# Key and value rows in groups of nine tokens: 64-row matmul pairs for the kv sums of a linear attention with an MLP behind it

## The chip, the cores and the metric

The kernel runs on one core of one Trainium2 chip. The metric is the device time of the whole kernel in microseconds (us): the time before is 294.24 us, the median of three runs (293.79 to 294.32).

## The reference

All inputs and the output are float32. There are 8 batches, 8 heads, 576 tokens and a head width of 64; the MLP goes from 512 to 2048 and back to 512.

```python
B, H, S, D = q.shape                                  # 8, 8, 576, 64
theta = np.pi / 2.0 * np.arange(S) / S
phi(x) = concat([relu(x) * cos(theta), relu(x) * sin(theta)], axis=-1)   # 128 wide
kv  = einsum('bhsf,bhsd->bhfd', phi(k), v)
z   = sum(phi(k), axis=2)
num = einsum('bhsf,bhfd->bhsd', phi(q), kv)
den = einsum('bhsf,bhf->bhs', phi(q), z)[..., None] + 1e-06
x   = (num / den).transpose(0, 2, 1, 3).reshape(B * S, H * D)           # 4608 x 512
out = leaky_relu(x @ w_in, 0.01) @ w_out                                 # 4608 x 512
```

The kv sum runs over the tokens of one batch and head, in any order. It gives a 128 x 64 matrix; two columns of ones beside v (so 66 columns, `NE`) give z with it.

## The kernel before, in words

A batch has 576 = 512 + 64 tokens. The first 512 are the main part (`MAIN`): partition p holds the four tokens 4p to 4p+3 (`J = 4`), so that one load moves runs of 4 x 64 floats (1024 bytes). The last 64 are the tail: two heads lie on top of each other, one in partitions 0 to 63 and one in 64 to 127, and a tail is loaded in two halves, in runs of 256 bytes. So k and v of one batch take one main load (two halves for batches 0 and 1) and two tail loads each. The main loads go into the `stage` pool (seven buffers, shared with the loads of q and of the weights, which are cast to f16 from there), the tails of k and v into `kvtail` (four buffers). `kpm` and `kpt` (pool `kpp`, two buffers) hold phi(k) of main part and tail in f16; `vmain` and `vtail` hold v in f16, with the ones, in two copies that take turns.

phi is written half by half (`phi_half`): on VectorE (DVE, L226) one instruction does the max with 0 and the product with cos or sin, a column with one value for each partition; on ScalarE (ACT, L224) it is a Relu with a scale. `k_main` does one of the four tokens, cos and sin half, over all eight heads (512 elements in each partition) or four heads (256); `k_tail` does the tail. `v_main` and `v_tail` copy v to f16.

The kv sum has two forms. Batches 0 and 1 do it in halves of four heads (`kv_half`, `kv_mm`): for each pair of heads one matmul of the tail (128 rows, 132 columns, L264; the zeros of `vtail` keep the two heads apart) and eight of the main part (128 rows, 66 columns, L274). Batches 2 to 7 do it at once (`kv_all`): eight tail matmuls of 64 rows (L290), which take the upper and the lower partitions in turn and write to two PSUM banks, then 32 of 128 rows (L299). ACT copies the sum to `kv` (L306, L315). `num` multiplies phi(q) by it (L373, or in halves L409), DVE divides (`divide`: L384, L388, L389), and x is transposed to `xT`.

The MLP runs over groups of 512 tokens: eight groups are the main parts of the eight batches, the ninth holds the tails of q of all batches. `ffn1` (L452) makes a pair of 128-row blocks of the hidden layer with 8 matmuls of 512 columns into a PSUM buffer of `ps_h` (two buffers); ACT takes leaky relu of the pair into `g` (L460; pool of two buffers). `ffn2` (L475) multiplies by w_out; DVE or ACT copies the result to `osb`, and SyncE (SP) stores it.

The order is written out by hand; each engine works in the order of the code. From group 1's middle on, a list of units (ffn1 of the next group and ffn2 of this one in turn, at positions that count 16 to a group) is woven with steps at positions of their own (`at`, `weave`): a step is put out before the first unit whose position is not smaller. `kv_steps` puts the work on k and v and the kv sum there, `load_steps` the loads, `q_steps` phi of q with its transposes by DMA. All loads, stores and DMA transposes wait in SP's one queue, and each waits for the eighth DMA before it to land.

Of the kernel before, what the change touches and what calls it, by code (L numbers as in the profile page):

```python
# [14 lines left out]
J = 4  # L15


@with_exitstack
def kernel(
# [22 lines left out]
    assert TAIL == P // 2 and B * TAIL == MAIN  # L42
    NKC = DM // P
# [6 lines left out]
    def pool(name, bufs, space=None):  # L50
        kw = {"space": space} if space is not None else {}
        return ctx.enter_context(tc.tile_pool(name=name, bufs=bufs, **kw))
# [4 lines left out]
    kvtail = pool("kvtail", 4)  # L57
    qtail = pool("qtail", 2)
    kppool = pool("kpp", 2)
# [21 lines left out]
    def load_main(nm, src, b, parts=(0, 1)):  # L81

        if parts[0] == 0:
            st[nm, b] = stage.tile([P, H, J, D], dt.float32, name=f"{nm}st", tag="stage")
        lo, hi = 4 * parts[0], 4 * parts[-1] + 4
        nc.sync.dma_start(  # L86
            st[nm, b][:, lo:hi],
            src[b, lo:hi, 0:MAIN, :].rearrange("h (p j) d -> p h j d", j=J),
        )

    def load_kvtail(nm, src, b):

        t = kvtail.tile([P, H // 2, D], dt.float32, name=f"{nm}tl", tag="kvtail")
        v4 = src[b, :, MAIN:S, :].rearrange("(c o) p d -> o p c d", o=2)
        for o in range(2):
            nc.sync.dma_start(t[o * TAIL : (o + 1) * TAIL], v4[o])  # L96
        st[nm + "t", b] = t
# [9 lines left out]

    def load_k(b):
        load_main("k", k, b)
        load_kvtail("k", k, b)  # L110

    def load_v(b):
        load_main("v", v, b)
        load_kvtail("v", v, b)
# [31 lines left out]
    load_kvtail("k", k, 0)  # L146
    load_main("k", k, 0, (0,))
    load_kvtail("v", v, 0)
# [32 lines left out]
    pos = const.tile([P, J + 1], dt.float32, name="pos")  # L181
# [15 lines left out]
    cos_t = const.tile([P, J + 1], dt.float32, name="cos_t")  # L197
    sin_t = const.tile([P, J + 1], dt.float32, name="sin_t")
# [5 lines left out]
    ones = const.tile([P, H, J, 2], dt.float32, name="ones")  # L204
    nc.vector.memset(ones, 1.0)
    vmain, vtail = [], []
    for i in range(2):
        vm = const.tile([P, H, J, NE], dt.float16, name=f"vmain{i}")
        nc.vector.tensor_copy(vm[:, :, :, D:NE], ones)

        vt = const.tile([P, H // 2, 2, NE], dt.float16, name=f"vtail{i}")
        nc.gpsimd.memset(vt, 0.0)
        for o in range(2):
            sl = slice(o * TAIL, (o + 1) * TAIL)
            nc.vector.tensor_copy(vt[sl, :, o, D:NE], ones[sl, 0:4, 0, :])
        vmain.append(vm)
        vtail.append(vt)
# [18 lines left out]
    def kp_tiles(b):  # L236
        st["kpm", b] = kppool.tile([P, H, J, F], dt.float16, name="kpm")
        st["kpt", b] = kppool.tile([P, H // 2, F], dt.float16, name="kpt")

    def k_main(b, j, eng_c, eng_s, lo=0, hi=H):  # L240
        kpm, kst = st["kpm", b], st["k", b]
        for eng, t, f in ((eng_c, cos_t, 0), (eng_s, sin_t, D)):
            phi_half(
                eng, kpm[:, lo:hi, j, f : f + D], kst[:, lo:hi, j, :], t[:, j : j + 1]
            )

    def k_tail(b, eng_c, eng_s):
        kpt, kt, c = st["kpt", b], st["kt", b], J
        phi_half(eng_c, kpt[:, :, 0:D], kt, cos_t[:, c : c + 1])
        phi_half(eng_s, kpt[:, :, D:F], kt, sin_t[:, c : c + 1])  # L250

    def v_main(b, lo, hi, eng):
        copy(eng, vmain[b % 2][:, lo:hi, :, 0:D], st["v", b][:, lo:hi])

    def v_tail(b, eng):
        for o in range(2):
            sl = slice(o * TAIL, (o + 1) * TAIL)
            copy(eng, vtail[b % 2][sl, :, o, 0:D], st["vt", b][sl])

    def kv_mm(b, hg, ps):  # L260
        kpm, kpt = st["kpm", b], st["kpt", b]
        for cc in range(2):
            c = 2 * hg + cc
            nc.tensor.matmul(  # L264
                ps[:, 2 * cc * NE : 2 * (cc + 1) * NE],
                lhsT=kpt[:, c, :],
                rhs=vtail[b % 2][:, c].rearrange("p a e -> p (a e)"),
                start=True,
                stop=False,
            )  # L270
            for o in range(2):
                h = 2 * c + o
                for j in range(J):
                    nc.tensor.matmul(  # L274
                        ps[:, (2 * cc + o) * NE : (2 * cc + o + 1) * NE],
                        lhsT=kpm[:, h, j, :],
                        rhs=vmain[b % 2][:, h, j, :],
                        start=False,
                        stop=(o == 1 and j == J - 1),
                    )  # L280

    def kv_all(b):

        ps = psum("n", [P, 2, 512], dt.float32, "ps_kv")[:, :, 0 : 4 * NE]
        ps = ps.rearrange("p o (c e) -> p o c e", c=4)
        kpm, kpt = st["kpm", b], st["kpt", b]
        for c in range(H // 2):
            for o in range(2):
                sl = slice(o * TAIL, (o + 1) * TAIL)
                nc.tensor.matmul(  # L290
                    ps[:, o, c],
                    lhsT=kpt[sl, c, :],
                    rhs=vtail[b % 2][sl, c, o, :],
                    start=(c == 0),
                    stop=False,
                )
        for h in range(H):
            for j in range(J):
                nc.tensor.matmul(  # L299
                    ps[:, h % 2, h // 2],  # L300
                    lhsT=kpm[:, h, j, :],
                    rhs=vmain[b % 2][:, h, j, :],
                    start=False,
                    stop=(h >= H - 2 and j == J - 1),
                )
        nc.scalar.copy(kv[b].rearrange("p (c o) e -> p o c e", o=2), ps)  # L306

    def kv_half(b, hg, where, out=True):
        st["kvh", hg] = psum(where, [P, 4 * NE], dt.float32, "ps_kvh")
        kv_mm(b, hg, st["kvh", hg])  # L310
        if out:
            kv_half_out(b, hg)

    def kv_half_out(b, hg):
        nc.scalar.copy(  # L315
            kv[b][:, 4 * hg : 4 * hg + 4].rearrange("p h e -> p (h e)"), st["kvh", hg]
        )
# [213 lines left out]
    kp_tiles(0)  # L531
# [4 lines left out]
    k_tail(0, DVE, DVE)  # L536
    v_tail(0, POOL)
    k_main(0, 0, ACT, DVE, 0, 4)
    for j in range(1, J):
        k_main(0, j, DVE, DVE, 0, 4)  # L540
    v_main(0, 0, 2, DVE)
    v_main(0, 2, 4, ACT)
# [4 lines left out]
    kv_half(0, 0, "o")  # L547
    for j in range(J):
        k_main(0, j, ACT, DVE, 4, 8)
    num_half(0, 0, 0, "h")  # L550
    num_half(0, 1, 0, "n")
    v_main(0, 4, 6, ACT)
    v_main(0, 6, 8, POOL)
    idle(6)
    x_transpose_half(0, 0, 0)
    kv_half(0, 1, "o")
# [28 lines left out]
    load_kvtail("k", k, 1)  # L585
    load_kvtail("v", v, 1)
    load_main("k", k, 1, (0,))
    load_w2(3, 0, 2)
    load_main("v", v, 1, (0,))
    load_w2(3, 2, 4)  # L590
    load_main("k", k, 1, (1,))
    load_main("v", v, 1, (1,))
    load_main("q", q, 2)
    load_k(2)
    load_v(2)
# [18 lines left out]
    def at(pos, f, *args):  # L614
        steps.append((pos, lambda: f(*args)))
# [14 lines left out]
    kp_tiles(1)  # L630
    k_tail(1, DVE, DVE)
    v_tail(1, DVE)
    for j in range(J):
        k_main(1, j, DVE, DVE, 0, 4)
    cast_w2(3, DVE, 0, 2)
    v_main(1, 0, 2, DVE)
# [9 lines left out]
    v_main(1, 2, 4, ACT)  # L646
    kv_half(1, 0, "h")
    for j in range(J):
        k_main(1, j, ACT, DVE, 4, 8)
# [4 lines left out]
    v_main(1, 4, 6, POOL)  # L654
    v_main(1, 6, 8, ACT)
# [5 lines left out]
    kv_half(1, 1, "h")  # L661
# [41 lines left out]
    def kv_steps(b, start, step, mm, eng_v, n_act=0):  # L703
        at(start - 0.01, kp_tiles, b)
        at(start, k_tail, b, DVE, DVE)
        for i in range(J):
            at(start + (i + 1) * step, k_main, b, i, ACT if i < n_act else DVE, DVE)
        v0, dv = (start + 1.5 * step, 1) if b > 3 else (start + 3 * step, 0.1)
        at(v0, v_main, b, 0, 4, eng_v)
        at(v0 + dv, v_main, b, 4, 8, eng_v)  # L710
        at(v0 + 2 * dv, v_tail, b, eng_v)
        at(mm, kv_all, b)

    def load_steps(b, pk, pv, pq):
        at(pk, load_k, b)
        at(pv, load_v, b)
        at(pq, load_main, "q", q, b)
# [13 lines left out]
    kv_steps(2, 9.7, 0.5, 14, DVE, 2)  # L731
# [6 lines left out]
    kv_steps(3, 20, 0.7, 24, ACT)  # L738
# [3 lines left out]
    kv_steps(4, 28, 1.2, 34, ACT)  # L742
# [3 lines left out]
    for b in range(5, NG):  # L746
        base = 16 * (b - 2)
        if b < B:
            load_steps(b, base - 14.5, base - 13, base - 14.6)
            kv_steps(b, base - 8, 1.2, base - 2, ACT)  # L750
        else:
            for j in range(J):
                at(base - 11.5 + 2 * j, load_qtail, j)
        q_steps(b, base - 8, 2, 1)
        out_steps(b, base + 1, 2, 1.6)
# [32 lines left out]
```

## Time and profile before

| | |
|---|---|
| median of three runs | 294.24 us (293.79 to 294.32) |
| the profiled execution's own time | 293.82 us |
| its span in the profile | 292.0 us |
| TensorE (PE) matmuls | busy 286.4 us, 98%, 1958 instructions |
| VectorE (DVE) | busy 128.7 us, 44%, 328 instructions |
| ScalarE (ACT) | busy 118.4 us, 41%, 148 instructions |
| GpSimd (POOL) | busy 12.7 us, 4%, 24 instructions |
| DMA | 87909 packets, 56.93 MB |

The profiled execution takes 1.8 us more than its span, for what lies ahead of and behind it. It is 0.42 us under the median of the runs. Matmul durations in the profile overlap (a matmul of 512 columns is 379 ns long, but the next one starts 216 ns later), so PE's pace is read from the starts. The granted clock is full in all forty slices.

### The profile page before, as it was taken

To read this page: it belongs to the slowest core of one execution; us is meant where nothing else is said; L and a number is where in the kernel's file an instruction comes from. 1 tells how busy PE (TensorE), PEld (TensorE's weight loads), DVE (VectorE), ACT (ScalarE), POOL (GpSimd) and SP (SyncE) were. 2 spreads that over 40 slices of the span, in tenths; PEclk is the share of its full clock that TensorE was granted. 3 is DMA by queue.
4 is the path that set the end of the run, shared out by engine and by line. 5 is a ranking of instruction groups with operands and counts; after the bars stand their busy time and mean duration, and the time that the engine had idled before them with its cause. 6 is when DMAs were issued, how large, how long until landed. Compare 5 with 4: busy or idle time off the path is not lost.

```text
span 292.0 us, 4774 instructions
## 1 busy us (share of the span) xinstructions
PE 286.4 (98%) x1958; PEld 152.7 (52%) x1958; DVE 128.7 (44%) x328; ACT 118.4 (41%) x148; POOL 12.7 (4%) x24
## 2 busy tenths in 40 slices
PE   8999999999999999999999999999999999999995
PEld 3585556555555555455545554555445444444444
DVE  6931687926835816823562356333323310000011
ACT  6865266753544632632263226322222222222200
POOL 2264000000000000000000000000000000000000
PEclk9999999999999999999999999999999999999999
DMA  7999999999999999789584989504691051011133
GB/s 233 348 386 407 325 364 335 315 204 324 212 241 318 229 291 298 166 162 338 164 182 84 296 233 199 91 37 110 160 199 38 36 108 38 36 54 54 39 71 73
DMA packets 87909, 56.93 MB, mean 195 GB/s; under 512 B 55888, under 2 KB 80720, under 8 KB 87504
## 3 DMA queue, kind: packets, MB, share of 16 engines
q1 hardware_dynamic: 87808, 56.57, 71.0%
q8 instruction: 15, 0.25, 0.4%
q10 hardware_dynamic: 80, 0.07, 0.1%
q14 instruction: 6, 0.05, 0.1%
HBM read 36.70 MB, written 9.44 MB: 158 GB/s over the span
## 4 chain that ended last, share of the span: by engine, by line
PE 94%; DMA 2%; SPq 1%; ACT 1%; DVE 1%; issue 0%
PE ps_h L452 43%; PE ps_o L475 41%; PE ps_num L373 3%; PE ps_kv L299 2%; DMA vst<-in_v_dram 2%; PE ps_l L504 1%; SPq L96 1%; PE ps_xth L425 1%; PE ps_qt L363 1%; PE ps_numh L409 1%; SPq L86 1%; PE ps_kv L290 0%; PE ps_idle L166 0%; PE ps_kvh L274 0%; ACT qpT L232 0%; PE ps_xt L438 0%
## 5 line engine op out<-in xcount | busy, mean ns | idle before, releaser
L452 PE MATMUL ps_h<-xT,w 128*128 128x512 f16 (+1 forms) x592 | 142.8, 373 | 0.1
L475 PE MATMUL ps_o<-w,g 128*128 128x512 f16 x560 | 139.5, 379 | 0.0
L460 ACT ACTIVATE g<-ps_h 128x1024 f16<-128x1024 f32 x72 | 73.2, 1023 | 128.8 <-PE ps_h L452 128.8
L452 PEld LDWEIGHTS <-w 128*128 128x128 f16 x592 | 64.4, 114 | 52.3 <-issue 0.2
L475 PEld LDWEIGHTS <-g 128*128 128x128 f16 x560 | 54.2, 98 | 61.4
L234 DVE COPY osb<-ps_o 128x512 f32<-128x512 f32 x31 | 21.4, 690 | 77.1 <-PE ps_o L475 75.3
L384 DVE TENSOR_SCALAR den<-ps_num 128x8 f32<-128x8 f32 x28 | 4.6, 165 | 54.9 <-PE ps_num L373 54.9
L389 DVE TENSOR_TENSOR xs<-ps_num,rden 128x512 f16<-128x512 f32 x28 | 19.4, 691 | 1.2 <-DVE rden L388 0.2
L226 DVE TENSOR_SCALAR kpm<-kst,sin_t 128x512 f16<-128x512 f32 (+1 forms) x40 | 16.6, 429 | 1.1 <-DMA kst<-in_k_dram 1.1
L226 DVE TENSOR_SCALAR qp<-qst,cos_t 128x512 f16<-128x512 f32 (+1 forms) x34 | 15.5, 456 | 2.8 <-DMA qst<-in_q_dram 2.8
L226 DVE TENSOR_SCALAR qp<-qst,sin_t 128x512 f16<-128x512 f32 (+1 forms) x34 | 15.5, 456 | 0.0
L373 PEld LDWEIGHTS <-qpT 128*128 128x128 f16 (+1 forms) x256 | 10.6, 101 | 7.3 <-issue 1.7
L232 ACT CAST vmain<-vst 128x1024 f16<-128x1024 f32 (+1 forms) x14 | 12.5, 920 | 2.4 <-DMA vst<-in_v_dram 2.3
L226 DVE TENSOR_SCALAR kpm<-kst,cos_t 128x512 f16<-128x512 f32 (+1 forms) x29 | 13.1, 453 | 0.3 <-DMA kst<-in_k_dram 0.3
L373 PE MATMUL ps_num<-kv,qpT 128*128 128x66 f16 (+1 forms) x256 | 11.8, 194 | 0.0
L166 PE MATMUL ps_idle<-blank 128*128 128x512 f16 x30 | 9.9, 478 | 1.2 <-DVE blank L161 1.2
L234 DVE CAST w<-w2st 128x1024 f16<-128x1024 f32 (+1 forms) x6 | 5.1, 868 | 11.8 <-DMA w2st<-in_moe_w_out_dram 11.8
L232 ACT COPY qpT<-ps_qt 128x1024 f16<-128x1024 f16 x7 | 7.0, 1012 | 5.7 <-PE ps_qt L363 5.7
L234 POOL CAST w<-w1st 128x1024 f16<-128x1024 f32 (+1 forms) x9 | 8.5, 945 | 3.6 <-DMA w1st<-in_moe_w_in_dram 3.6
L388 DVE RECIPROCAL rden<-den 128x8 f32<-128x8 f32 x36 | 7.3, 203 | 1.2
L299 PE MATMUL ps_kv<-vmain,kpm 128*128 128x66 f16 x192 | 7.1, 193 | 0.0
L299 PEld LDWEIGHTS <-kpm 128*128 128x128 f16 x192 | 6.4, 98 | 0.3
(62 smaller groups left out, 99.7 us busy)
## 6 DMA issues: line engine op xcount, KB each, us to landing
out_dram<-osb SPq DMA_DIRECT2D x32, 256.0 KB, 2.5
qst<-in_q_dram SPq DMA_DIRECT2D x7, 1024.0 KB, 6.8
kst<-in_k_dram SPq DMA_DIRECT2D x6, 1024.0 KB, 9.7
vst<-in_v_dram SPq DMA_DIRECT2D x6, 1024.0 KB, 9.4
w1st<-in_moe_w_in_dram SPq DMA_DIRECT2D x7, 512.0 KB, 10.4
w2st<-in_moe_w_out_dram SPq DMA_DIRECT2D x3, 1024.0 KB, 12.9
kst<-in_k_dram SPq DMA_DIRECT2D x4, 512.0 KB, 6.9
vst<-in_v_dram SPq DMA_DIRECT2D x4, 512.0 KB, 7.9
```

Of the source, the lines that this page charges most:

```text
L166: nc.tensor.matmul(ps, lhsT=blank[:, 0:P], rhs=blank)
L226: eng.tensor_scalar(out=o, in0=i, scalar1=0.0, scalar2=col, op0=ALU.max, op1=ALU.mult)
L232: nc.scalar.copy(o, i)
L234: eng.tensor_copy(o, i)
L299: nc.tensor.matmul(ps[:, h % 2, h // 2], lhsT=kpm[:, h, j, :], rhs=vmain[b % 2][:, h, j, :], start=False, stop=(h >= H - 2 and j == J - 1),)
L373: nc.tensor.matmul(ps[lo:hi, h // 4, (h % 4) * NE : (h % 4 + 1) * NE], lhsT=qpT[:, h, lo:hi], rhs=kv[b][:, h, :],)
L384: nc.vector.tensor_scalar_add(den.rearrange("p (a b) -> p a b", a=2), ps[:, :, D : 4 * NE : NE], 1e-6)
L388: nc.vector.reciprocal(rden, den)
L389: nc.vector.tensor_tensor(out=xs, in0=ps[:, :, 0 : 4 * NE].rearrange("p a (b e) -> p a b e", e=NE)[:, :, :, 0:D], in1=rden.rearrange("p (a ...
L452: nc.tensor.matmul(ps[:, m % 2, lo:hi], lhsT=w1[m // 4, c][0][:, w1[m // 4, c][1], m % 4 : 512 : 4], rhs=xT[:, lo // P : hi // P, c, :], s ...
L460: nc.scalar.activation(st["g", g][:, m - 1 : m + 1, :], ps, AF.Lrelu)
L475: nc.tensor.matmul(st["ps_o", g, tt], lhsT=st["g", g][:, m, tt * P : (tt + 1) * P], rhs=w2[:, m, :], start=(m == 0), stop=(m == NFT - 1),)
```

## The change

From batch 1 on, k and v have no main part and tail. 576 = 64 x 9, so partition p of 64 holds the nine tokens 9p to 9p+8 (`T = 9`), and the 128 partitions hold two heads on top of each other (`HP = 64`, `NC = 4` pairs of heads). One load moves runs of 9 x 64 floats (2304 bytes) for the whole batch; batch 1 has two halves of two pairs each. The tail loads of batches 1 to 7, their copies of v and their phi of k are gone.

phi of k is now done for each of nine tokens over four pairs (`k_token`: 256 elements), so 18 instructions for a batch in place of 8 of 512 and 2 of 256. Batch 1 does it another way: pair by pair, one DVE instruction for nine tokens (576 elements) with the table of cos or sin as a second tensor (`k_pair_half`), for pairs 0 and 1 and for the sin half of pairs 2 and 3; the cos half of pairs 2 and 3 goes token by token (128 elements), five on ACT and four on DVE. v is cast in two copies of 1152 elements a batch (four of 576 in batch 1) to `vm`, two copies that take turns.

`kv_sum` has for each pair of heads and each token two matmuls of 64 rows, upper and lower partitions, into two PSUM banks: 72 for a batch in place of 40 (batches 2 to 7) or 36 (batch 1, in two calls of 36 now).

`kpp` has one buffer in place of two, and the pool `kvtail` is gone: the tails of batch 0's k and v go through a buffer of `qtail`. Batch 0 keeps its form; its `kpm`, `kpt`, `vmain` and `vtail` lie in the first buffer of the pool of `g`, which group 1's hidden layer takes later. The stage buffers grow from 2048 to 2304 elements. Positions in `kv_steps` are set anew: nine steps of half the length in place of five.

```diff
+T = 9
-    kvtail = pool("kvtail", 4)
-    kppool = pool("kpp", 2)
+    kppool = pool("kpp", 1)
+    def load_kv(nm, src, b, parts=(0, 1)):
+        if parts[0] == 0:
+            st[nm, b] = stage.tile([P, NC, T, D], dt.float32, name=f"{nm}st", tag="stage")
+        sl = slice(2 * parts[0], 2 * parts[-1] + 2)
+        rows = src[b].rearrange("h s d -> (h s d)").rearrange("(c p x) -> p c x", c=NC, p=P)
+        nc.sync.dma_start(
+            st[nm, b][:, sl].rearrange("p c j d -> p c (j d)"), rows[:, sl]
+        )
...
+    scratch = gpool.tile([P, NFT, MAIN], dt.float16, name="g").rearrange("p m t -> p (m t)")
...
+    def k_token(b, j, eng, t, f, lo=0, hi=H // 2):
+        c = J + 1 + j
+        phi_half(
+            eng, st["kp", b][:, lo:hi, j, f : f + D], st["k", b][:, lo:hi, j, :],
+            t[:, c : c + 1],
+        )
...
+    def k_pair_half(b, c, t, f):
+        nc.vector.scalar_tensor_tensor(
+            out=st["kp", b][:, c, :, f : f + D],
+            in0=st["k", b][:, c],
+            scalar=0.0,
+            in1=t[:, J + 1 :][:, :, None].broadcast_to([P, T, D]),
+            op0=ALU.max,
+            op1=ALU.mult,
+        )
...
+    def kv_sum(b, lo, hi, where):
+        n = hi - lo
+        ps = psum(where, [P, 2, 512], dt.float32, "ps_kv")
+        for c in range(lo, hi):
+            for j in range(T):
+                for o in range(2):
+                    sl = slice(o * HP, (o + 1) * HP)
+                    nc.tensor.matmul(
+                        ps[:, o, (c - lo) * NE : (c - lo + 1) * NE],
+                        lhsT=st["kp", b][sl, c, j, :],
+                        rhs=vm[b % 2][sl, c, j, :],
+                        start=(j == 0),
+                        stop=(j == T - 1),
+                    )
...
-    load_kvtail("k", k, 1)
-    load_kvtail("v", v, 1)
-    load_main("k", k, 1, (0,))
+    load_kv("k", k, 1, (0,))
     load_w2(3, 0, 2)
-    load_main("v", v, 1, (0,))
+    load_kv("v", v, 1, (0,))
     load_w2(3, 2, 4)
...
-    v_main(1, 2, 4, ACT)
-    kv_half(1, 0, "h")
-    for j in range(J):
-        k_main(1, j, ACT, DVE, 4, 8)
+    v_pairs(1, 1, 2, ACT)
+    kv_sum(1, 0, 2, "h")
+    for c in range(2, 4):
+        k_pair_half(1, c, sin_t, D)
+    for j in range(T):
+        k_cos(1, j, ACT if j < 5 else DVE, 2, 4)
     ffn2_mm(0, 2, 12, 14)
...
     def kv_steps(b, start, step, mm, eng_v, n_act=0):
-        at(start - 0.01, kp_tiles, b)
-        at(start, k_tail, b, DVE, DVE)
-        for i in range(J):
-            at(start + (i + 1) * step, k_main, b, i, ACT if i < n_act else DVE, DVE)
-        v0, dv = (start + 1.5 * step, 1) if b > 3 else (start + 3 * step, 0.1)
-        at(v0, v_main, b, 0, 4, eng_v)
-        at(v0 + dv, v_main, b, 4, 8, eng_v)
-        at(v0 + 2 * dv, v_tail, b, eng_v)
-        at(mm, kv_all, b)
+        at(start - 0.01, kp_tile, b)
+        for j in range(T):
+            at(start + j * step, k_cos, b, j, ACT if j < n_act else DVE)
+            at(start + j * step, k_sin, b, j, DVE)
+        v0, dv = (start + 3 * step, 1) if b > 3 else (start + 6 * step, 0.1)
+        at(v0, v_pairs, b, 0, 2, eng_v)
+        at(v0 + dv, v_pairs, b, 2, 4, eng_v)
+        at(mm, kv_sum, b, 0, NC, "n")
...
-    kv_steps(2, 9.7, 0.5, 14, DVE, 2)
+    kv_steps(2, 9.7, 0.25, 14, DVE, 4)
```

## The prediction

> **What bounds the kernel now.** I read the page first (busy shares, granted clock), then the chain of waits, then the time line around one kv sum, and last the starts of single matmuls.
>
> ```profile
> PE 286.4 (98%) x1958; PEld 152.7 (52%) x1958; DVE 128.7 (44%) x328; ACT 118.4 (41%) x148; POOL 12.7 (4%) x24
> PEclk9999999999999999999999999999999999999999
> PE 94%; DMA 2%; SPq 1%; ACT 1%; DVE 1%; issue 0%
> L299 PE MATMUL ps_kv<-vmain,kpm 128*128 128x66 f16 x192 | 7.1, 193 | 0.0
> L299 PEld LDWEIGHTS <-kpm 128*128 128x128 f16 x192 | 6.4, 98 | 0.3
> ```
>
> PE is busy for 98% at full clock and makes up 94% of the chain. Busy alone would prove little, so I took the distance from each matmul's start to the next and subtracted what the same form takes when nothing interferes (216 ns for 512 columns, 56 for 128, about 32 for 66). Over the whole run 6.6 us are left over, of which 4.4 lie in the first 20 us (k, q and v of batch 0 landing), 0.53 between 40 and 50 us, 0.24 between 50 and 60, and 1.4 in all that follows. From 20 us to the end PE's stream is therefore nearly gapless, and the change costs what it adds to that stream, plus what it makes PE wait for. Faster loads can win only parts of those 0.8 us, since batch 0 is not touched.
>
> The time line of PE around the sum of batch 2, and the engines around it:
>
> ```profile
> 60.63 0.29 PE L290 MATMUL ps_kv<-vtail,kpt 64*128 64x66 f16 x8
> 60.85 1.19 PE L299 MATMUL ps_kv<-vmain,kpm 128*128 128x66 f16 x32
> 61.88 0.38 PE L452 MATMUL ps_h<-xT,w 128*128 128x512 f16 x1
> 54.69 1.94 ACT L460 ACTIVATE g<-ps_h 128x1024 f16<-128x1024 f32 x2
> 56.50 1.35 ACT L224 ACTIVATE kpm<-kst,cos_t 128x512 f16<-128x512 f32 x2
> 57.72 1.03 ACT L460 ACTIVATE g<-ps_h 128x1024 f16<-128x1024 f32 x1
> ```
>
> The first three lines show that the 64-row form is already there: eight tail matmuls in 0.22 us. The other three show ACT without a break from 54.69 to 58.75, which matters below.
>
> **The kv sums of batches 2 to 7, on the path.** Single starts of that sum, in ns after the regular place of the next matmul: 96 until the first tail matmul, then pairs of an upper and a lower one 3 or 4 ns apart, the pairs at 0, 38, 74 and 103; then 124 until the first 128-row matmul; then 31 distances between the 32, of which the first are 39, 35 and 33 and the long run is 32.2; 33 more to the next 512-column matmul. The two long distances, 96 and 124, are the change between 64 and 128 rows: about 90 ns more than a step each. All six sums agree within 5 ns, 1.35 us each.
>
> After it there are 36 pairs. The way in stays (96). The second change of form moves from between tail and main part to the end (124). Between lie 35 distances: the first three cost 103 as in the tails, the other 32 at 32.2 give 1030. The sum is 96 + 103 + 1030 + 124 = 1353 ns, as much as before: 32 more matmuls cost nothing as long as a pair goes at the pace of one 128-row matmul. The trace shows only four pairs in a row. Bounds: 29 ns (the last distance of the four) gives -0.1 us a sum, 34.3 (the mean of the three) +0.07; over six sums -0.6 to +0.4. I take 0, as the three distances behind a change of form are slow in both forms (103 against 107).
>
> Here the Trainium skill speaks against the change: its page "TensorE: Matmul & The Clock Gate", section "Wait — 56ns, not 53.3ns?", has starts of matmuls never closer than about 25 ns. By that rule, as an estimate, 72 matmuls would take 1.8 us, and six sums 3.8 us more than I count. The pairs here start 3 to 4 ns apart, so the trace differs from it for upper and lower rows; the row decides.
>
> **Batch 1, on the path.** Its halves had no 64-row matmuls (L264, L274): 2 x 57 + 16 x 32.2 = 0.63 us. Now each is 96 + 103 + 14 x 32.2 + 124 = 0.77 us, so +0.15. Behind the first half PE waits 0.2 us today, from 43.96 to 44.16, as the halves of `num` need ACT's copy of the sum (L315, 0.38 us) and only two 512-column matmuls lie between. The change of form at the end (90 ns) falls into that wait. So +0.06 and +0.15: +0.2 us.
>
> **ACT in batch 2, on the path.** `kv_steps` gave ACT two cos tokens of 512 elements; now it gets four of 256. Two of the former take 1.23 us (56.50 to 57.72 above); four of the latter took 1.61 us from first start to the next instruction in batches 0 and 1 (L224: 12.14 to 13.75 and 44.77 to 46.38). ACT is 0.38 us later with the next leaky relu, which in the trace ends at 58.75; PE's matmul that takes its buffer in `ps_h` starts at 58.81, 0.06 us later than the pace wants, so there is no slack. The order of the new kernel puts the four at the same place, between the third and the fourth leaky relu of group 1. +0.38 us.
>
> **DVE, beside PE.** For a batch it now has 18 phi instructions of 256 elements at a distance of 0.262 us, 4.72 us, in place of 8 at 0.395 and 2 at 0.262, 3.68 us: +1.04 us. Where does that fit? Batch 2: five DVE tokens do both halves and four one, 3.67 us, with v copies of 1152 elements some 1.34 more; it ends near 59.7, and PE gets there at 60.6. Batch 3: DVE is dense from 75.03 to 80.4 and PE starts the sum at 81.16; now it ends near 81.4, and the last token is needed by the ninth pair, 0.3 us into the sum: no slack left, no loss either. Batch 4: it waits for the tail of k until 92.61 and is dense until 100.6, PE starts at 100.8. k now lands as one load at about 91.9, where the main part landed at 91.96; the work ends near 101.0, the ninth pair is at 101.1. Batches 6 and 7: three tokens behind the copy at 150.57 and 180.59, where two of 512 elements were: the same end. Margins of 0.1 us are no margins, so I count 0.1 us for all of it, between 0 and 0.4.
>
> Batch 1's four instructions for pairs 0 and 1 have no row of their form; nearest is the division's product L389, two tensors and 512 elements, 0.61 us from start to start. For 576 that is 0.68, so 2.7 us where phi and v tails took 3.2. Work on pairs 0 and 1 then ends no later than now (42.4, needed 42.9). Bounds: at half the rate it is +2.7 us and PE stands 2 us; at twice, nothing is won, because PE does not wait there.
>
> **Loads and what costs nothing.** A tensor of a batch had 1024 packets of 1024 bytes (median 48 ns each) and 512 of 256 bytes (18 ns): 58 us over 16 engines, 3.6 us. 512 packets of 2304 bytes, at 85 ns for 2048 some 95, make 3.0 us. SP has four issues fewer a batch. So k and v of batch 1 land about 1.4 us earlier, but behind 20 us PE waits for no load that is not covered: the cover is DVE's 0.3 to 1.3 us of lead above, and without these earlier loads the cos and sin halves of pairs 2 and 3 (two of 0.68 and four of about 0.2, where four of 0.262 were) would hold the division and PE by up to 1 us. The front: two more iotas end near 2.0 us, ahead of the cos table at 2.95; one memset less; DVE's preparations end before q lands at 4.6. Zero. One buffer of `kpp` is written at the earliest four positions (7 us) after the sum that reads it; group 1 takes batch 0's scratch 35 us later.
>
> **The sum.** 0 + 0.2 + 0.38 + 0.1 = +0.7 us on the profiled execution's 293.82: 294.5. The median of the runs lies 0.42 above that execution, so I expect a median of 294.9 against 294.24. About 0.2%, 0.59 us, is what a measurement of this kernel can tell from no change; the bounds are 293.65 and 294.83. By its own terms (-0.6 to +0.4 for the pairs, 0 to 0.4 for DVE) this case reaches from 294.3 to 295.6.
>
> **Rivals.** (a) The pairs run dry. A sum of 72 matmuls and as many weight loads follows a stretch with 216 ns for each two; whatever waits ahead of PE is used up. Only 40 in a row are seen, at full pace. If from the 33rd matmul on they went one after another at 32.2 ns, 40 matmuls would take 1.29 us in place of 0.64, +0.65 us in each of six sums, a little in batch 1: +4 us, 298.9. It costs something from the point at which a matmul with its load needs over 16 ns. For it: no trace of long pairs; against it: the four pairs show no slowing. The same section of the Trainium skill has a mode in which the sequencer takes about 62 ns for a matmul, which as an estimate would make it +1.8 us a sum and 306; no run here shows that pace.
> (b) DVE is late in batch 1 by the two-tensor form or by loads that gain less than 1.4 us: +0.5 to +2 us, 295.5 to 297.
> (c) The other side: pairs at 29 ns save 0.1 us in 6 sums and the two halves (-0.7), leaving form at the end hides behind the following 512-column matmul's weight load (90 ns, -0.5 in six), and the earlier loads take away half of the 0.8 us around batch 1 (-0.4): from +0.7 to -0.9, 293.4. It decides from about 30 ns a pair. For it: the 29 ns; against it: all single matmuls' long run at 32.2.
> (d) ACT's four tokens find cover, the rest as in my sum: +0.3, 294.5, no measurable change.
>
> **Numbers.** My case 0.50, of which about 0.33 is beyond 0.2% and 0.17 within; (a) 0.16; (b) 0.13; (c) 0.15; (d) 0.06. Slower 0.62, same 0.23, faster 0.15. The likeliest is 294.9. The range takes (d), most of (b) and the mild part of (a), and leaves out most of (c) and the hard part of (a): 293.9 to 297.2.
>
> **What would show it.** In the new profile: the distance of pairs far into a sum (32 ns right; 50 to 64 is (a), 29 is (c)); one sum from regular place to next 512-column matmul 1.35 us; PE's start behind the fourth leaky relu of group 1 late by 0.4 us; no PE wait ahead of batch 1's sums, k landing near 43.3 for the second half; 0.2 us or less ahead of the sums of batches 3 and 4. The prediction is wrong if the sums differ from 1.35 us by over 0.1, or if PE's lost time lies at a place not named here.

## The result and the profile after

The changed kernel takes 295.71 us (median of 10 runs, 295.11 to 296.56), the kernel before 294.62 us in the same comparison (10 runs, 293.79 to 295.26). The ratio is 1.0038, with a 95% interval of 1.002 to 1.0055: slower, by 0.6 to 1.6 us. The profiled execution took 296.38 us, with a span of 294.4 us, which is 2.6 and 2.4 us more than the one shown of before.

From the page of the changed kernel, the same parts as before: busy time, clock, the chain's shares by engine, and the groups of the kv sum.

```profile
PE 287.2 (98%) x2186; PEld 152.8 (52%) x2186; DVE 134.0 (46%) x365; ACT 115.7 (39%) x141; POOL 14.3 (5%) x25
PEclk9999999999999999999999999999999999999999
PE 92%; ACT 2%; DMA 2%; SPq 1%; DVE 1%; issue 0%; ACTq 0%
L356 PEld LDWEIGHTS <-kp 64*128 64x128 f16 x504 | 8.5, 94 | 3.4 <-issue 1.7
L356 PE MATMUL ps_kv<-vm,kp 64*128 64x66 f16 x504 | 9.5, 191 | 0.0
```

PE executes 228 more matmuls and is busy only 0.8 us longer. The chain now gives ACT 2% where it had 1%. That points away from the sums, but busy shares prove little here; the starts of single matmuls decide. The time line of ACT, then of PE, around the sum of batch 2:

```profile
55.29 2.86 ACT L509 ACTIVATE g<-ps_h 128x1024 f16<-128x1024 f32 x3 [1.28 <-PE ps_h L501]
58.02 1.71 ACT L254 ACTIVATE kp<-kst,cos_t 128x256 f16<-128x256 f32 x4
59.62 1.94 ACT L509 ACTIVATE g<-ps_h 128x1024 f16<-128x1024 f32 x2
```

```profile
58.62 1.67 PE L501 MATMUL ps_h<-xT,w 128*128 128x512 f16 x7
60.69 1.89 PE L501 MATMUL ps_h<-xT,w 128*128 128x512 f16 x8 [0.40 <-ACT g L509]
62.51 1.32 PE L356 MATMUL ps_kv<-vm,kp 64*128 64x66 f16 x72
63.76 1.05 PE L501 MATMUL ps_h<-xT,w 128*128 128x512 f16 x4
```

ACT's four tokens run from 58.02 to the next leaky relu at 59.62, 1.60 us, and PE stands at 60.69 for a buffer of `ps_h`. The 0.40 is idle time beside the modelled ends; by single starts the wait is 558 ns against 58 ns in the profile before. The third line of PE is a whole sum in its new form: 72 matmuls, 1.35 us from the regular place of the next matmul to the next 512-column one.

To see where the time went, I compare the place of the same MLP matmul in both traces, counted from the span's start: the 33rd of `ps_h` (end of the front), the 90th (behind batch 1's sums), the 180th (behind those of batches 2 and 3), and the last. The differences between them, in ns against the profile shown of before:

| kernel | front | batch 1 | batches 2, 3 | rest |
|---|---|---|---|---|
| before, first profile | 0 | 0 | 0 | 0 |
| before_again | -161 | +550 | -3 | 0 |
| changed kernel | +1160 | +224 | +597 | +79 |
| after_again | +180 | +221 | +606 | +78 |
| act_two | +463 | +219 | +41 | +79 |
| act_none | +269 | +219 | -18 | +78 |
| before_act_split | -91 | +690 | +370 | +6 |
| extra_before | -64 | +1712 | +1 | +10 |
| extra_after | +457 | +224 | +594 | +78 |
| front_only | +909 | +3 | +145 | +9 |
| tails_only | +655 | +3 | +1 | +6 |
| scratch_only | +1079 | 0 | +137 | +6 |
| rows_apart | +406 | +699 | +1437 | +1590 |
| split_sums | +594 | +225 | +602 | +934 |

Behind the front the changed kernel loses 0.90 us, in both of its profiles the same; to this come 0.25 us behind the last matmul (below). The front varies from execution to execution, and so does batch 1 in the kernel before.

### The profile page after: what moved, and what is told of

Read it like the earlier page. It is cut to its first block, busy times and chain, and to the rows that moved or that the text cites. A ratio compares the mean times of both kernels' runs of the same rounds, so it can differ in the third digit from the quotient of the medians.

```text
span 294.4 us, 5216 instructions
## 1 busy us (share of the span) xinstructions
PE 287.2 (98%) x2186; PEld 152.8 (52%) x2186; DVE 134.0 (46%) x365; ACT 115.7 (39%) x141; POOL 14.3 (5%) x25
## 4 chain that ended last, share of the span: by engine, by line
PE 92%; ACT 2%; DMA 2%; SPq 1%; DVE 1%; issue 0%; ACTq 0%
PE ps_o L524 41%; PE ps_h L501 41%; PE ps_kv L356 3%; PE ps_num L422 3%; DMA vst<-in_v_dram 2%; ACT g L509 1%; PE ps_l L553 1%; SPq L102 1%; PE ps_xth L474 1%; PE ps_qt L412 1%; ACT kp L254 1%; SPq L90 1%; PE ps_numh L458 1%; PE ps_idle L174 0%; ACT qpT L262 0%
## 5 line engine op out<-in xcount | busy, mean ns | idle before, releaser
L256 DVE TENSOR_SCALAR kp<-kst,cos_t 128x256 f16<-128x256 f32 (+1 forms) x54 | 18.6, 348 | 0.0
L256 DVE TENSOR_SCALAR kp<-kst,sin_t 128x256 f16<-128x256 f32 x54 | 18.4, 346 | 0.0
L262 ACT CAST vm<-vst 128x1152 f16<-128x1152 f32 (+1 forms) x12 | 12.4, 1069 | 0.0
L356 PEld LDWEIGHTS <-kp 64*128 64x128 f16 x504 | 8.5, 94 | 3.4 <-issue 1.7
L356 PE MATMUL ps_kv<-vm,kp 64*128 64x66 f16 x504 | 9.5, 191 | 0.0
L363 ACT CAST kv<-ps_kv 128x528 f16<-128x528 f32 (+1 forms) x8 | 4.4, 544 | 10.5 <-PE ps_kv L356 10.5
```

Source lines behind the costliest of these rows:

```text
L256: eng.tensor_scalar(out=o, in0=i, scalar1=0.0, scalar2=col, op0=ALU.max, op1=ALU.mult)
L262: nc.scalar.copy(o, i)
L356: nc.tensor.matmul(ps[:, o, (c - lo) * NE : (c - lo + 1) * NE], lhsT=st["kp", b][sl, c, j, :], rhs=vm[b % 2][sl, c, j, :], start=(j == 0), ...
L363: nc.scalar.copy(kv[b].rearrange("p (c o) e -> p o c e", o=2)[:, :, lo:hi, :], ps[:, :, 0 : n * NE].rearrange("p o (c e) -> p o c e", c=n),)
```

## The experiments

Each ratio is to the kernel before, run on the same chip in the same comparison.

**after_again**: the changed kernel without an edit, for the repeat of its profile.

> The changed kernel once more, for a second profile. Theory: PE loses 0.2 us in batch 1, 0.5 us behind the fourth leaky relu of group 1 and nothing in the sums of batches 2 to 7; what the first profile lost beyond that before 20 us (1.2 us) was one late DMA engine and need not come again: +0.6 to +1.1 us over the kernel before, and v of batch 0 may land near 10.4 us again. Rival: the new arrangement of batch 0 is itself slower, v of batch 0 lands 1 us late in every profile of it: +1.5 us or more.

Measured: 295.44 us against 294.53, ratio 1.0037 (1.002 to 1.0055). The profile repeats batch 1, the wait for ACT (564 ns) and the rest to within 10 ns, and shows 1.0 us less in the front: +0.18. What is in the table's three right columns belongs to the change; most of the front's 1.16 us did not come back.

**act_two**: two of the four tokens of batch 2 that ACT had go to VectorE.

```diff
-    kv_steps(2, 9.7, 0.25, 14, DVE, 4)
+    kv_steps(2, 9.7, 0.25, 14, DVE, 2)
```

> The changed kernel, but in batch 2 ACT takes two cos tokens of 256 elements and DVE the other seven. Theory: ACT is done 0.8 us earlier with its tokens, the wait of PE behind the fourth leaky relu (0.56 us) is gone, so 0.5 us less than the changed kernel. Rival: the wait is for something else (the transposes, the loads of batch 2), then no difference; or DVE's two more tokens delay the sum of batch 2, then PE waits there instead.

Measured: 294.84 against 294.53, ratio 1.0021 (1.001 to 1.0031). ACT's time line:

```profile
57.32 0.92 ACT L254 ACTIVATE kp<-kst,cos_t 128x256 f16<-128x256 f32 x2
58.11 1.03 ACT L509 ACTIVATE g<-ps_h 128x1024 f16<-128x1024 f32 x1
59.63 1.02 ACT L509 ACTIVATE g<-ps_h 128x1024 f16<-128x1024 f32 x1 [0.49 <-PE ps_h L501]
```

Now ACT waits for PE behind the fourth leaky relu, not PE for ACT: the last line has 0.49 us of idle time put down to PE. The column for batches 2 and 3 falls from +0.60 to +0.04. The loss came from ACT's row of instructions ahead of that leaky relu being too long.

**before_act_split**: the kernel before, with each of ACT's two cos tokens of batch 2 cut into two of 256 elements, the elements of the changed kernel's four tokens without anything else of the change.

```diff
-            at(start + (i + 1) * step, k_main, b, i, ACT if i < n_act else DVE, DVE)
+            at(start + (i + 1) * step, k_split if i < n_act else k_main, b, i, ACT if i < n_act else DVE, DVE)
```

`k_split` does the cos half of a token in two instructions of four heads.

> The kernel before, but in batch 2 each of ACT's two cos tokens of 512 elements is done as two of 256. Theory: this alone brings the wait behind the fourth leaky relu: PE starts 0.4 to 0.5 us late there, +0.4 us over the kernel before. Rival: the wait needs the new layout or the new order of steps, then no difference.

Measured: 294.94 against 294.53, ratio 1.0023 (1.001 to 1.0035).

```profile
57.10 1.71 ACT L224 ACTIVATE kpm<-kst,cos_t 128x256 f16<-128x256 f32 x4
58.69 1.94 ACT L469 ACTIVATE g<-ps_h 128x1024 f16<-128x1024 f32 x2
```

The same 1.59 us of ACT, and a wait of 419 ns, 0.36 more than before: the stall comes with the split alone. The changed kernel's 0.50 has 0.14 more, which scratch_only explains below. The same profile holds a surprise: batch 1, which the edit does not touch, is 0.69 us later than in the first profile, because its loads landed 0.6 us later. PE stood 206, 282 and 180 ns ahead of and behind its sums.

**before_again**: the kernel before without an edit, to see whether that comes by itself.

> The kernel before once more, for a second profile of it. Theory: no wait behind the fourth leaky relu beyond 0.2 us and 0.2 us ahead of the halves of num in batch 1; where a DMA engine is late, either the front is longer or batch 1 loses up to 0.7 us. Rival: the first profile is typical and nothing of that shows.

Measured: 294.23 us in one run, beside a median of 294.32 us for that kernel on the same chip. The front is 0.16 us earlier than in the first profile, and batch 1 loses 0.55 us. VectorE's sin halves of batch 1's second half wait for k:

```profile
45.20 1.14 DVE L226 TENSOR_SCALAR kpm<-kst,sin_t 128x256 f16<-128x256 f32 x4 [0.81 <-DMA kst<-in_k_dram]
```

and PE, by single starts, stands 78, 267 and 181 ns ahead of its matmuls at 42.88, 47.44 and 48.47 us, where the first profile has no gap. So the kernel before does lose time to loads in batch 1, and its first profile did not show it. Together with the three kernels with a late front, in which batch 1 loses nothing (0 to +3 ns), the picture fits one bound: batch 1 can't go before its loads, and a late front only uses up the wait. That reading is from the table; no run set the front's time by itself.

**extra_before** and **extra_after**: either kernel with two loads of 256 KB ahead of batch 1's k and v, into buffers that nothing reads.

```diff
     load_w2(2)
+    for c in range(2):
+        spare = opool.tile([P, DM], dt.float32, name="osb", tag="osb")
+        nc.sync.dma_start(spare, w1v[:, c, 0:512])
```

> The kernel before with two loads of 256 KB more that nobody reads (weight columns into two buffers of osb), ahead of the loads of k and v of batch 1, which land some 1.3 us later. Theory: in this kernel the loads of batch 1 have no cover: phi of k, the division and the second half of the sum come late, PE loses 0.7 to 1.5 us between 42 and 50 us. Rival: they are covered, 0 to 0.2 us.

> The changed kernel with the same two loads more at the same place. Theory: here k and v of batch 1 land about 1.4 us earlier than in the kernel before, so the delay uses up that lead and no more: 0 to 0.2 us over the changed kernel. Rival: the earlier landing is no lead, because DVE's two-tensor instructions need it: 0.7 us or more, as in the kernel before.

Measured: the kernel before with them 296.43 against 294.24, ratio 1.0072 (1.0055 to 1.0088; the profiled execution, at 295.63, was the fastest of the five); the changed kernel with them 295.43, ratio 1.0048 (1.003 to 1.0067). PE in batch 1's first half, first of the kernel before, then of the changed kernel, and its VectorE:

```profile
42.84 0.22 PE L264 MATMUL ps_kvh<-vtail,kpt 128*128 128x132 f16 x1
44.13 0.41 PE L274 MATMUL ps_kvh<-vmain,kpm 128*128 128x66 f16 x8 [1.07 <-DVE vmain L234]
```

```profile
40.77 2.75 PE L524 MATMUL ps_o<-w,g 128*128 128x512 f16 x12
43.46 0.74 PE L356 MATMUL ps_kv<-vm,kp 64*128 64x66 f16 x36
44.13 0.60 PE L524 MATMUL ps_o<-w,g 128*128 128x512 f16 x2
```

```profile
37.44 0.76 DVE L336 SCALAR_TENSOR_TENSOR kp<-kst,cos_t 128x576 f16<-128x576 f32 x1 [0.72 <-DMA kst<-in_k_dram]
42.81 1.43 DVE L336 SCALAR_TENSOR_TENSOR kp<-kst,sin_t 128x576 f16<-128x576 f32 x2 [0.74 <-DMA kst<-in_k_dram]
```

The kernel before pays 1.71 us in batch 1 of its profiled execution. In the changed kernel VectorE waits for k in both halves, PE goes on without a gap, and batch 1 costs the same +0.22 us as without the loads. The second half of k lands at 42.79 us here and at 41.55 in the changed kernel's first profile, against 44.75 in the kernel before. The earlier landing covers this delay of about 1.2 us in full; where nothing delays the loads, it is worth what the kernel before happens to lose, 0 to 0.7 us. With the same extra loads the changed kernel is the faster one by 1.0 us in the medians, though the two intervals overlap.

**front_only**: the kernel before, with the new place of batch 0's k, v and tails alone.

```diff
+    scratch = gpool.tile([P, NFT, MAIN], dt.float16, name="g").rearrange("p m t -> p (m t)")
...
+        if b == 0:
+            if "tails" not in st:
+                st["tails"] = qtail.tile([P, H, D], dt.float32, name="qtl", tag="qtail")
```

> The kernel before with the change of batch 0 alone: its phi(k), v and their tails lie in the first buffer of g's pool, the tails of k and v are loaded into a buffer of qtail. Theory: no difference beyond 0.3 us, and where one of the 16 DMA engines is late in the profile, it is at another place. Rival: this arrangement costs what the changed kernel lost ahead of 20 us, about 1 us.

Measured: 294.44 against 294.53, ratio 1.0005 (0.9993 to 1.0017): no cost that can be measured, in the kernel before. Its profile still has the front 0.91 us late. In the trace one of the sixteen DMA engines lands its share of the first half of v at 11.32 us, the first engine at 9.75; in the kernel before all sixteen lie between 9.80 and 10.41. The changed kernel's first profile has it more strongly (9.01 to 11.66); its ACT copy of v starts 1.3 us later than before:

```profile
11.68 0.62 ACT L262 CAST g<-vst 128x512 f16<-128x512 f32 x1 [1.78 <-DMA vst<-in_v_dram]
```

**tails_only** and **scratch_only**: the two parts of front_only, each alone.

> The kernel before with one part of the new front: the tails of k and v of batch 0 go through one buffer of the pool of q's tails in place of two of their own pool. In the four profiles with the old batch 0 all sixteen DMA engines land their share of the first v half within 0.3 to 0.6 us of each other (9.80 to 9.96 first, 10.25 to 10.41 last). If the two tails sharing a tile cause the single late engine, the distance is over 0.9 us and the dense run of the first hidden layer starts at 15.6 us or later; if the place of phi(k) and v in the tile of g does, it stays at 0.6 us or less and 15.3 to 15.5 us. If it is the placement of the packets by chance, neither kernel shows it or both do.

> The kernel before with the other part of the new front: phi(k) and v of batch 0 in the first buffer of g, tails in their own pool as before. If the tile of g is the cause (other addresses for the f16 copies that run while the loads land, two more DVE copies and one POOL memset at the start), the distance between first and last engine of the first v half is over 0.9 us and the dense run starts at 15.6 us or later; if the tails are, 0.6 us or less and 15.3 to 15.5 us.

Measured, one run each: 294.51 and 295.05 us, beside 294.48 for the kernel before. First and last engine are 1.33 us apart with the tails moved and 1.65 us with the scratch moved (two engines late there); the front is 0.66 and 1.08 us late. Both show it, so it does not hang on one of the two parts alone. Single packets of 1024 bytes, whose usual time is 46 to 48 ns, take 0.2 to 1.2 us around 7.4 to 10 us in every kernel with any part of the new front, in after_again too, where that load landed in time, at 9.80 us; in three of the four profiles without it none does, in the fourth two. The cause stays open.

The two part at another place: scratch_only loses 0.14 us in batches 2 and 3, as front_only does, and tails_only nothing. ACT in tails_only, then in scratch_only:

```profile
54.43 2.85 ACT L465 ACTIVATE g<-ps_h 128x1024 f16<-128x1024 f32 x3 [1.14 <-PE ps_h L457]
57.16 1.34 ACT L229 ACTIVATE kpm<-kst,cos_t 128x512 f16<-128x512 f32 x2
```

```profile
54.99 2.85 ACT L481 ACTIVATE g<-ps_h 128x1024 f16<-128x1024 f32 x3 [1.28 <-PE ps_h L473]
57.71 1.35 ACT L242 ACTIVATE kpm<-kst,cos_t 128x512 f16<-128x512 f32 x2
```

The first leaky relu of group 1 waits 1.28 us after ACT's last work in place of 1.14. Against PE's matmuls it starts 0.137 us later. The single instructions say why: where g's first buffer held batch 0's scratch, ACT executes two waits on semaphores as instructions of their own ahead of this leaky relu: the one for PE's matmuls at 54.85 us (released at 54.83), and one at 54.90 us for work of VectorE and ACT that was over by 54.17. The leaky relu then starts at 54.99. In tails_only its only wait, the one for PE, is part of the leaky relu itself. ACT has no gap from there to the fourth leaky relu, so PE's wait grows from 58 to 194 ns (198 in front_only). The changed kernel has the same two waits.

**rows_apart**: the changed kernel with the loop over the two halves of rows outside the loop over tokens, so that nine upper matmuls are followed by nine lower ones.

```diff
-            for j in range(T):
-                for o in range(2):
+            for o in range(2):
+                for j in range(T):
```

> The changed kernel, but in each kv sum the nine matmuls of the upper rows of a pair of heads come first and then the nine of the lower rows, in place of taking turns. Same matmuls, same number. Theory: two matmuls overlap only when they follow one another in different halves; now each takes about the 32 ns that a pair took: a sum of batches 2 to 7 goes from 1.35 to about 2.3 us, the halves of batch 1 from 0.77 to 1.25, +6 to +7 us over the changed kernel. Rival: a 64-row matmul is cheap by itself (16 ns), the order does not matter, no difference.

Measured: 298.27 against 294.24, ratio 1.0135 (1.0119 to 1.015). The sum of batch 2:

```profile
62.24 1.70 PE L356 MATMUL ps_kv<-vm,kp 64*128 64x66 f16 x72
```

A sum takes 1.72 us, not the 2.3 that would come if nothing overlapped. Of every nine distances between starts in the middle of the sum, two are 29 to 33 ns and seven 8 to 25 ns; the mean of all 71 is 21.2 ns. In turn it is 15.9. So nine matmuls on one half of the rows still overlap in part with the nine that follow on the other half. The overlap of upper and lower rows is what lets 72 matmuls cost no more than 40, and taking turns is worth 0.37 us a sum.

**split_sums**: from batch 4 on two calls of two pairs, with one unit of the MLP between.

```diff
+            at(mm, kv_sum, b, 0, 2, "n")
+            at(mm + 0.5, kv_sum, b, 2, NC, "n")
```

> The changed kernel, but batches 4 to 7 do their kv sum in two calls of two pairs of heads, with one unit of four 512-column matmuls between them. Four more changes to 64 rows and back. Theory: each costs 96 ns in, 90 out and 26 behind the first wide matmul, 0.21 us, so +0.85 us over the changed kernel, +1.9 over the one before. Rival: the change of form is hidden or happens once for nearby calls, then no difference.

Measured: 296.29 against 294.24, ratio 1.0074 (1.0057 to 1.009).

```profile
102.23 0.74 PE L356 MATMUL ps_kv<-vm,kp 64*128 64x66 f16 x36
102.91 1.05 PE L501 MATMUL ps_h<-xT,w 128*128 128x512 f16 x4
103.90 0.74 PE L356 MATMUL ps_kv<-vm,kp 64*128 64x66 f16 x36
```

The halves take 770 to 776 ns each. The four batches lose 0.86 us more than in the changed kernel, 0.21 us for one more change to 64 rows and back. The two halves of a batch together take 0.20 us more than its whole sum: 96 ns on the way in, 90 on the way out, and some 10 for pairs that are slow behind a change of form. The rest lies behind the exit, where the second 512-column matmul starts late: 242 to 245 ns after the first, in place of 216, at five of these eight exits and at those of the changed kernel's whole sums, 226 at the other three.

**act_none**: no token on ACT in batch 2, and batch 3's steps earlier.

```diff
-    kv_steps(2, 9.7, 0.25, 14, DVE, 4)
+    kv_steps(2, 9.7, 0.25, 14, DVE, 0)
-    kv_steps(3, 20, 0.35, 24, ACT)
+    kv_steps(3, 19.2, 0.4, 24, ACT)
```

> The changed kernel with two of its losses taken away: ACT takes no cos token of batch 2 (DVE does all nine), and the steps of batch 3 begin 0.8 positions earlier. Theory: the wait behind the fourth leaky relu (0.56 us) and the wait in the sum of batch 3 (0.05 us) are gone, so 0.6 us less than the changed kernel; what stays is 0.2 us in batch 1 and 0.13 us in the exits of the six sums: about +0.3 us over the kernel before where that one's loads are in time, no difference that can be measured. Rival: DVE with all of batch 2 is late for its sum, and 0.3 us or more of wait comes back there.

Measured: 294.57 against 294.32, ratio 1.0003 (0.9986 to 1.002). ACT behind its third and fourth leaky relu:

```profile
57.71 1.02 ACT L509 ACTIVATE g<-ps_h 128x1024 f16<-128x1024 f32 x1 [0.46 <-PE ps_h L501]
59.44 1.02 ACT L509 ACTIVATE g<-ps_h 128x1024 f16<-128x1024 f32 x1 [0.70 <-PE ps_h L501]
```

ACT waits for PE in both, all sums of batches 2 to 7 take 1345 to 1348 ns, and behind the front only 0.28 us are left of the 0.90: batch 1's forms and the exits, less the 58 ns of wait that the kernel before has behind the fourth leaky relu. This version leaves no loss that can be measured, and it does not beat the kernel before.

## Why the prediction was right

The forecast was 294.9 us and slower; the median came out at 295.71, inside the range and 0.1 us beyond the 295.6 that its own case reached, with the kernel before at 294.62 in place of 294.24. Of its two signs of being wrong the first did not show: the sums differ from 1.35 us by at most 0.05. The second did in part: PE also loses time behind the exits and after the last matmul, which the prediction does not name. The steps, in its order:

- **The kv sums of batches 2 to 7**: right. Five of them take 1344 to 1349 ns from place to place, against 1350 to 1357 before and 1353 in the sum; the two of a pair start 2 to 5 ns apart and pairs repeat every 32 ns to the 36th. Batch 3's takes 1400, for another reason (below). The rule on about 25 ns between starts (the Trainium skill's page "TensorE: Matmul & The Clock Gate", section "Wait — 56ns, not 53.3ns?") does not hold for upper and lower rows in turn: 15.9 ns in the mean over 72. Its mode of 62 ns a matmul is not seen here.
- **The change of form**: the 26 to 29 ns behind each exit are missing from the sum. Before, the exit lay inside the sum between tail and main part, now a 512-column matmul follows it. Over six sums this is 0.12 us, less than six times 26 because each sum itself is up to 10 ns shorter than before.
- **Batch 1's halves**: 772 to 773 ns each, as predicted (0.77), and 0.22 us in all, as predicted (0.2).
- **ACT in batch 2**: the mechanism and place were right, the term was mis-sized: 0.50 for 0.38. The part of it that was predicted is 0.36 (the split alone). The other 0.14 are the two semaphore waits that stand as instructions of their own ahead of group 1's first leaky relu where the scratch is in g's buffer. The prediction let that go with "group 1 takes batch 0's scratch 35 us later": nothing had to be waited for, but the waits themselves are instructions, on an engine without slack.
- **VectorE**: 0.05 us in batch 3, nothing elsewhere, inside the 0 to 0.4. The last sin half runs from 82.97 to 83.32; by single starts the ninth pair of the sum, the first that needs it, starts at 83.38, 76 ns behind the pair before it where some 32 is the rule. The sum itself begins on time. The 0.42 us ahead of its weight loads is not this wait: it stands in act_none too (third line), whose sum of batch 3 loses nothing.

```profile
82.97 0.35 DVE L256 TENSOR_SCALAR kp<-kst,sin_t 128x256 f16<-128x256 f32 x1
83.06 1.25 PEld L356 LDWEIGHTS <-kp 64*128 64x128 f16 x72 [0.42 <-DVE kp L256]
81.61 1.19 PEld L356 LDWEIGHTS <-kp 64*128 64x128 f16 x72 [0.42 <-DVE kp L256]
```

- **The two-tensor form**: 0.68 us apart were estimated, 0.67 it is, and the work ends before PE needs it.

```profile
36.70 0.75 DVE L336 SCALAR_TENSOR_TENSOR kp<-kst,cos_t 128x576 f16<-128x576 f32 x1
37.37 0.75 DVE L336 SCALAR_TENSOR_TENSOR kp<-kst,sin_t 128x576 f16<-128x576 f32 x1
41.57 1.43 DVE L336 SCALAR_TENSOR_TENSOR kp<-kst,sin_t 128x576 f16<-128x576 f32 x2 [0.25 <-DMA kst<-in_k_dram]
```

- **"Behind 20 us PE waits for no load that is not covered"**: wrong in general, right only for the profile it was read from. Two other profiles of the old batch 1 lose 0.55 and 0.69 us there. So the earlier loads (k's second half 3.2 us, not 1.4) pay back part of what the change costs.
- **The front at zero**: not so in the traces. In all ten profiles with the new front or a part of it the front is 0.18 to 1.16 us late (0.46 in the middle one of the seven with the whole change), in the three others with the old one 0.06 to 0.16 us early. The time of front_only does not settle it, because in the kernel before, by the reading above, a late front uses up the wait for loads in batch 1. The changed kernel has no such wait: its batch 1 costs 0.22 us whether the front is 0.18 or 1.16 us late, so there a late front counts in full. No run has the changed kernel with the old front.
- **The end**: not in the sum at all. Behind the last matmul the changed kernel, act_two and act_none take 0.25 us longer, though the last landing comes at the same 2.91 us. SP (SyncE) goes through the semaphores in five steps in a fixed order, about 63 ns each. In the kernel before four of them are over when the last store lands; in the changed kernel, with 117 DMA issues in place of 145, the first step already waits for that landing, and all five follow it. With two more DMAs (the extra loads) the order shifts again: +0.15 us in the kernel before, -0.14 in the changed one.

The terms that repeat are 0.22 + 0.50 + 0.05 + 0.12 + 0.25 = 1.14 us, where 0.7 was forecast. To them comes the front (+0.18 and +1.16 in the two profiles), and off them goes what the kernel before loses in batch 1 (0 and 0.55). Together that is 0.8 to 2.3 us, which reaches beyond the measured 0.6 to 1.6, since the last two are seen only one execution at a time. The second profiles of the two kernels, whose executions lie nearer to the medians, differ by 0.96 us in span: 0.34 in the front, -0.33 in batch 1, 0.69 behind it and 0.26 after the last matmul. The balance is not proved to closer than that. That the forecast came near rests in part on the missed losses and the missed gain standing against each other.

The rivals: (a) fell, no pair is slower late in a sum. (b) fell, since the two-tensor form kept its pace and the loads gained more than 1.4 us. (c) fell in two of its three legs, since the long run of pairs is at 32 ns and the exit costs about 116 (90 and 26) in place of nothing; its third, the earlier loads, holds in some executions. (d) fell: ACT found no cover.

## What to carry to other kernels

Cutting the same elements into twice as many instructions can cost time (1.59 us in four where two took 1.22), and what decides is whether that engine has slack at that spot: here 0.4 us on ACT, 39% busy over the run, was paid in full by PE, and so were two semaphore waits of 0.14 us that came with a buffer's new tenant. One profile of a kernel shows which waits occurred, not which can: before calling a load covered, look at a second profile, or delay the load and see who waits. Here two 64-row matmuls on different halves of the rows cost no more than one of 128 rows (32 ns) if they take turns, but each change to this form and back costs about 0.2 us, so they belong in one stretch.

## What the hardware showed that I had not expected

Alternating 64-row matmuls overlap almost wholly (2 to 5 ns between the starts of a pair, 72 in a row), and even with nine on the same rows in a row the changes of rows still save time (21.2 ns a matmul where 32 was expected). With another number of DMA issues the end of this kernel changed by up to 0.25 us, through the order in which the last semaphores are checked. One or two DMA engines of sixteen can be 1 to 2 us behind the others in a load of 0.5 MB, and the load counts as landed only with them; packets of up to 1.2 us were seen around that time, but no run shows that they are the reason.
